# Finished rows stored from ScalarE's queue, the seventh page loaded by SyncE, and the experts' weights behind it

## The chip, the cores and the metric

The kernel runs on one core of one Trainium2 chip. The metric is the device time of one execution in microseconds: 382.13 us, the median of 3 runs of the kernel before (381.15 to 383.65). A page of a profile shows one execution, taken by the hardware profiler.

## The reference

The input is x of 8 batches, 2496 positions and 256 channels. Stage one mixes the positions of each batch by a filter in the frequency domain; stage two sends every position ("token") to one of 8 experts, of which each keeps its 80 tokens of highest gate weight, and puts them through two layers. All other rows of the output are zero.

```python
X = np.fft.rfft(x, axis=1)
Y = X * (filt_r + 1j * filt_i)[None]
t = np.fft.irfft(Y, n=2496, axis=1).reshape(19968, 256)
logits = t @ w_gate                                # 8 experts
expert_idx = argmax(logits); gate_w = softmax(logits)[expert_idx]
out = zeros((19968, 256))
for e in range(8):                                 # the 80 best tokens of expert e
    h = np.maximum(t[tok_idx] @ w1[e], 0.0)        # 256 -> 1024
    out[tok_idx] = gate_w[tok_idx, None] * (h @ w2[e])   # 1024 -> 256
```

## The kernel before

The kernel never makes all 19968 mixed rows. It makes the filtered spectrum of every batch, computes the gate's logits from the spectrum, chooses the tokens, and only for the chosen ones makes the rows themselves.

**The main loop** (up to about 233 us of the profile) transforms the batches by matmuls, multiplies by the filter, and writes each batch's spectrum, 2.6 MB, to a scratch tensor yf in DRAM; the last batch's spectrum stays in SBUF (yt_t). The output is zeroed by 32 stores in between.

**The rounds.** Behind the loop the chosen rows are made in seven rounds (NR) of up to 128 rows. Rounds 0 to 3 serve batches 0 to 3, one each; rounds 4 to 6 serve batches 4 to 7 in twelve groups of 32 rows, four groups to a round. For a round, GpSimd gathers rows of a table of cosines and sines by an indirect DMA (gather_rows, line 853, four for each round), VectorE turns them (turn_rows, line 864), and TensorE multiplies them with the "page" of the batch, the spectrum fetched back from yf into SBUF by four DMAs of 640 KB (load_page, line 838). `fill(n)` (line 876) issues the next n of a round's 20 steps. Round 5 takes rows of batches 5 and 6, round 6 of batches 6 and 7. At a round's end ScalarE copies the 128 finished rows out of PSUM (yr, one buffer; the tile z in round 5) and a DMA stores them to y_sel in DRAM (line 883).

**The experts** (function experts): the rows of each expert are gathered from y_sel by an indirect DMA (80 rows of 1 KB), turned by TensorE (px), and put through layer 1 (ph, line 1221) and layer 2 (po, line 1241); a scaled copy on ScalarE and an indirect DMA put them into the output. The first two experts' rows are gathered ahead (xg_first, line 1161), from the rounds 0 to 5 alone; the rows of round 6, still in SBUF, are added to them by a second matmul (line 1201). The others (xg_True, line 1188) are gathered from all of y_sel, the third expert's first. Expert 2's rows are turned in the middle of expert 0's layer 2 (`layer2(e, mid=lambda: turn(2))`).

**Weights.** w1 and w2 of an expert are 1 MB each, and each pair is fetched by two DMAs of SyncE (load_weights, lines 1066 and 1068) into one tile. The table WT names the buffer of each expert: its own tile, or the buffer of a page that its round has used up.

**What sets the order.** The work behind the loop is written under a manual schedule: each engine runs its instructions in the order in which the lines are written, and waits only for data and buffers. SyncE, ScalarE and GpSimd each issue DMAs on a queue of their own, in their own order; a DMA instruction that waits for data or a buffer holds up what stands behind it on its engine.

Of the kernel before, what the change touches and what calls it, by code (L numbers as in the profile page):

```python
# [13 lines left out]
F32 = mybir.dt.float32  # L14
# [5 lines left out]
B, S, C = 8, 2496, 256  # L20
# [13 lines left out]
E, FF = 8, 1024  # L34
NDB, NFC = C // 128, FF // 128
# [62 lines left out]
def kernel(  # L98
# [160 lines left out]
    with tc.manual_schedule():  # L259
# [608 lines left out]
        def fill(n):  # L868
            for _ in range(n):
# [9 lines left out]
                if s == NS - 1:  # L879
                    yr = (zs[:].rearrange("p e s -> p (e s)") if r == NR - 2 else  # L880
                          yr_p.tile([128, C], F32, name=f"yr_{r}", tag="yr"))
                    nc.scalar.copy(out=yr[:], in_=st["po"][:])  # L882
                    nc.sync.dma_start(
                        out=y_sel[128 * r:128 * r + 128, :], in_=yr[:])
                    st["yr"] = yr
# [164 lines left out]
        for name in ("t2", "pr", "fwd"):  # L1050
# [9 lines left out]
              (w_p, "w"), (last, "page"), (late, "page0")]  # L1060
        ws = {}

        def load_weights(e):
            where, tag = WT[e]
            ws[e] = where.tile([128, NDB * FF + NFC * C], F32, name=f"w_{e}", tag=tag)
            nc.sync.dma_start(out=ws[e][:, 0:NDB * FF].rearrange("p (k f) -> p k f", k=NDB),
                              in_=moe_w1[e].rearrange("(k p) f -> p k f", p=128))
            nc.sync.dma_start(out=ws[e][:, NDB * FF:].rearrange("p (k d) -> p k d", k=NFC),
                              in_=moe_w2[e].rearrange("(k p) d -> p k d", p=128))
# [3 lines left out]
        load_weights(0)  # L1073
# [23 lines left out]
        fill(2)  # L1097
# [10 lines left out]
        fill(7)  # L1108
# [5 lines left out]
        fill(13)  # L1114
        load_page(5, pg_p)
        load_weights(1)
# [17 lines left out]
        load_page(6, late, "page1", eng=nc.gpsimd)  # L1134
# [5 lines left out]
        fill(20)  # L1140
        turn_all(4)
# [13 lines left out]
        fill(10)  # L1155
        turn_all(6)
# [9 lines left out]
        for e in (3, 4):  # L1166
            load_weights(e)
# [13 lines left out]
    def experts(fp, psF, load, first):  # L1181
# [27 lines left out]
        def layer1(e, between=None):  # L1209
            w1 = ws[e][:, 0:NDB * FF].rearrange("p (k f) -> p k f", k=NDB)  # L1210
# [20 lines left out]
        def layer2(e, mid=None):  # L1231
            w2 = ws[e][:, NDB * FF:].rearrange("p (k d) -> p k d", k=NFC)
# [46 lines left out]
        for e in range(E):  # L1279
# [17 lines left out]
            n = e + 5 if first else e + 3  # L1297
# [12 lines left out]
    def general(tc, gctx):  # L1310
# [63 lines left out]
        def load(e):  # L1374
            ws[e] = wpool.tile([128, NDB * FF + NFC * C], F32, name=f"w2_{e}", tag="w")
            nc.sync.dma_start(out=ws[e][:, 0:NDB * FF].rearrange("p (k f) -> p k f", k=NDB),
                              in_=moe_w1[e].rearrange("(k p) f -> p k f", p=128))
            nc.sync.dma_start(out=ws[e][:, NDB * FF:].rearrange("p (k d) -> p k d", k=NFC),
# [415 lines left out]
```

## Time and profile before

| what | us |
| --- | --- |
| median of 3 runs | 382.13 |
| the profiled execution | 381.79 |
| its span, first to last instruction | 379.9 |
| TensorE busy | 352.4 |
| VectorE busy | 240.6 |
| GpSimd busy | 181.0 |
| ScalarE busy | 132.9 |

All times of the trace count from the span's start. PE is TensorE's matmul, PEld its weight load, DVE VectorE, ACT ScalarE, POOL GpSimd, SP SyncE; SPq and ACTq are the DMA issues of an engine. The names in the rows are the program's, with buffer numbers left out: gt are gathered rows of the table, wt the same rows turned, pr a round's sums in PSUM. A bracket behind a row tells how long the engine had been idle before it, and what released it. A float32 matmul shows as two rows of the trace.

### The profile page before, as it was taken

The numbers are of one execution on the slowest core, as the hardware profiler recorded it, in microseconds if no ns is written. First come the engines' busy times: TensorE is split into PE (matmuls) and PEld (weight loads), VectorE is DVE, ScalarE is ACT, GpSimd is POOL, SyncE is SP. The second block draws the span as 40 slices with busy tenths as digits, with TensorE's granted clock in tenths as the row PEclk, the third lists the DMA queues.
The fourth block names the chain that finished last, engine by engine and source line by source line (L and its number), as shares of the span: only waits on it lengthen the run. The fifth ranks groups of instructions, "written<-read, shape, count | busy, mean of one in ns | idle before, by whom it ended". The sixth has DMA issues, their size and how long they took to land. (4 is left out here: it accounts for less than half of the span.)

```text
span 379.9 us, 9671 instructions
## 1 busy us (share of the span) xinstructions
PE 352.4 (93%) x3941; PEld 312.5 (82%) x3941; DVE 240.6 (63%) x493; ACT 132.9 (35%) x275; POOL 181.0 (48%) x251
## 2 busy tenths in 40 slices
PE   8789999999999999999999999989899795997890
PEld 4789989989999899899899898778787363997880
DVE  6088666748868768789989887689947630121110
ACT  1445544554455455455354454150100000010110
POOL 8428455545545546646448858840283104022220
PEclk9999999999999999999999999999999998799997
DMA  7998698999989999989999999799999675989210
GB/s 220 282 340 262 207 331 263 321 305 305 346 274 303 369 265 326 333 235 310 348 295 271 394 296 335 270 405 388 416 406 399 222 249 166 332 286 363 88 31 12
DMA packets 41099, 109.92 MB, mean 289 GB/s; under 512 B 4202, under 2 KB 14312, under 8 KB 39176
## 3 DMA queue, kind: packets, MB, share of 16 engines
q1 hardware_dynamic: 36534, 95.94, 74.6%
q0 software_dynamic: 4240, 13.15, 9.7%
q8 instruction: 33, 0.54, 0.6%
q10 hardware_dynamic: 274, 0.14, 0.2%
q14 instruction: 18, 0.15, 0.1%
HBM read 70.42 MB, written 40.37 MB: 292 GB/s over the span
## 5 line engine op out<-in xcount | busy, mean ns | idle before, releaser
L360 POOL TENSOR_TENSOR yt<-p 128x256 f32<-128x256 f32 x157 | 113.6, 745 | 90.7 <-DVE p L352 87.4
L352 DVE TENSOR_TENSOR p<-pb,ft 128x1024 f32<-128x1024 f32 x80 | 97.0, 1215 | 42.1 <-issue 17.9
L316 PE MATMUL pa<-wf_t,x 117*128 117x120 f32 x704 | 90.6, 275 | 2.7 <-DMA x<-in_x_dram 1.8
L316 PEld LDWEIGHTS pa<-wf_t,x 117*128 117x128 f32 x704 | 84.5, 192 | 4.1 <-DMA x<-in_x_dram 1.4
L342 PE MATMUL pb<-d_t,t 128*128 128x128 f32 x640 | 84.7, 275 | 0.1
L342 PEld LDWEIGHTS pb<-d_t,t 128*128 128x128 f32 x640 | 77.8, 192 | 0.3 <-ACT t L335 0.3
L321 ACT COPY tt<-pa 128x480 f32<-128x480 f32 x96 | 47.9, 516 | 78.1 <-PE pa L316 77.0
L876 PE MATMUL pr<-page,wt 128*32 128x256 f32 (+1 forms) x520 | 64.5, 380 | 1.3 <-DVE wt L864 1.3
L876 PEld LDWEIGHTS pr<-page,wt 128*32 128x32 f32 (+1 forms) x520 | 46.4, 134 | 15.3 <-DVE wt L864 2.8
L335 ACT COPY t<-pt 128x512 f32<-128x512 f32 x80 | 47.2, 590 | 14.6 <-PE pt L331 12.6
L373 DVE STREAM_TRANSPOSE u<-yt 128x512 f32<-128x512 f32 x70 | 48.9, 699 | 0.0
L331 PE MATMUL pt<-ident,tt 128*128 128x128 f32 x320 | 48.6, 274 | 0.4 <-ACT tt L321 0.4
L853 POOL DMA_INDIRECT gt<-rows_tbl,idxr x28 | 29.8, 1064 | 33.9 <-DVE idxr L695 18.1
L331 PEld LDWEIGHTS pt<-ident,tt 128*128 128x128 f32 x320 | 37.3, 142 | 1.9 <-issue 1.2
L864 DVE STREAM_TRANSPOSE wt<-gt 128x640 f32<-128x640 f32 x28 | 22.7, 830 | 10.6 <-DMA gt<-rows_tbl,idxr 10.5
L1177 POOL DMA_INDIRECT out_dram<-ys_True,idxs x7 | 6.5, 933 | 34.8 <-ACT ys_True L1266 21.2
L396 PE MATMUL pz<-yt,wg 128*32 128x128 f32 (+1 forms) x256 | 21.9, 436 | 0.0
L882 ACT COPY yr<-pr 128x256 f32<-128x256 f32 x6 | 2.3, 380 | 54.9 <-PE misc L816 25.5
L1241 PE MATMUL po_True<-hT_True,w 128*64 128x80 f32 x448 | 17.9, 234 | 3.3 <-issue 3.3
L1221 PE MATMUL ph_True<-xs_True,w 128*64 128x80 f32 x512 | 20.9, 243 | 0.0
L1221 PEld LDWEIGHTS ph_True<-xs_True,w 128*64 128x64 f32 x512 | 20.0, 146 | 0.3 <-issue 0.2
L1241 PEld LDWEIGHTS po_True<-hT_True,w 128*64 128x64 f32 x448 | 16.3, 137 | 4.4 <-issue 3.8
(226 smaller groups left out, 287.4 us busy)
## 6 DMA issues: line engine op xcount, KB each, us to landing
out_dram<-zero_t SPq DMA_DIRECT2D x32, 624.0 KB
yf<-u SPq DMA_DIRECT2D x56, 320.0 KB, 5.3
w<-in_moe_w_dram SPq DMA_DIRECT2D x16, 1024.0 KB, 9.6
page<-yf SPq DMA_DIRECT2D x24, 640.0 KB, 9.5
x<-in_x_dram SPq DMA_DIRECT2D x16, 936.0 KB
x<-in_x_dram SPq DMA_DIRECT2D x7, 702.0 KB
page<-yf POOLq DMA_DIRECT2D x4, 640.0 KB, 8.7
fst<-in_filt_r_dram SPq DMA_DIRECT2D x10, 128.0 KB, 3.8
```

What stands on the lines that cost most here:

```text
L316: nc.tensor.matmul(out=ps[:, j, :], rhs=wf_t, start=True, stop=True, lhsT=xt[3 * b + ch][:, j0 + j - JC * ch, 128 * cb:128 * cb + 128])
L321: nc.scalar.copy(out=tt[h][:, :, H3 * j0:H3 * j0 + hn * jn].rearrange("p s (j h) -> p s j h", h=hn), in_=v)
L331: nc.tensor.transpose(ps[:, i, :], tt[h][:, 2 * s:2 * s + 2, :].rearrange("p r n -> p (r n)"), ident[:])
L335: nc.scalar.copy(out=t2[k][:], in_=ps[:])
L342: nc.tensor.matmul(out=ps[:, :, i, :], lhsT=t[:, i, :], rhs=d_t[:, SG * g + i, :], start=True, stop=True)
L352: nc.vector.tensor_tensor(out=p[:], in1=f.unsqueeze(2).to_broadcast(shape), op=AL.mult, in0=ps[:].rearrange("p r s q -> p r (s q)").unsque ...
L360: eng.tensor_tensor(out=y[:, :, 2 * r:2 * r + 2, :], in0=a, in1=b, op=op)
L373: nc.vector.transpose(uu[h][:, :, SG * g:SG * g + SG, :].rearrange("p a s w -> p s a w"), spectrum(h)[:, SG * g:SG * g + SG])
L853: nc.gpsimd.indirect_dma_start(out=gts[b, g][:].rearrange("p s q -> p (s q)"), out_offset=None, in_=quarters, in_offset=bass.IndirectOffse ...
L876: nc.tensor.matmul(st["po"][c:c + w, :], lhsT=wts[r][:, s, c:c + w], rhs=yt_t[:, :, s] if b == B - 1 else columns(pages[b], s), start=(s = ...
L1221: nc.tensor.matmul(ph[c:c + 64, i, 0:cap], lhsT=w1[:, k, f:f + 64], rhs=xs[:, k, :], start=(k == 0), stop=(k == NDB - 1))
L1241: nc.tensor.matmul(po[c:c + 64, d, 0:cap], lhsT=w2[:, fc, 128 * d + c:128 * d + c + 64], rhs=hT[:, fc, :], start=(fc == 0), stop=(fc == NF ...
```

## The change

- The store of a round's finished rows is issued by ScalarE, right behind its copy, and no longer by SyncE.
- The seventh page (of batch 6) is loaded by SyncE and no longer by GpSimd.
- The weights of expert 0 are loaded behind the seventh page and no longer ahead of the rounds; those of experts 1 to 5 stand behind rounds 3 to 6.
- Expert 5's weights get buffers of their own: its two halves lie in the two buffers of turned rows (pool u). Experts 6 and 7 take the buffers of experts 0 and 1 instead of 1 and 2.
- Four steps of round 1 stand ahead of the keys' turn to PSUM instead of behind it (fill 2, 7, 13 becomes 6, 5, 11).

```diff
@@ fill
                     nc.scalar.copy(out=yr[:], in_=st["po"][:])
-                    nc.sync.dma_start(
+                    nc.scalar.dma_start(
                         out=y_sel[128 * r:128 * r + 128, :], in_=yr[:])
@@ behind the loop
         WT = [(w_p, "w"), (last, "page"), (late, "page0"), (pg_p, "page"), (late, "page1"),
-              (w_p, "w"), (last, "page"), (late, "page0")]
+              None, (w_p, "w"), (last, "page")]
         ws = {}
 
         def load_weights(e):
-            where, tag = WT[e]
-            ws[e] = where.tile([128, NDB * FF + NFC * C], F32, name=f"w_{e}", tag=tag)
-            nc.sync.dma_start(out=ws[e][:, 0:NDB * FF].rearrange("p (k f) -> p k f", k=NDB),
+            if WT[e] is None:
+                ws[e] = [u_p.tile([128, NDB * FF], F32, name=f"w_{e}_{i}", tag="u")[:]
+                         for i in range(2)]
+            else:
+                where, tag = WT[e]
+                w = where.tile([128, NDB * FF + NFC * C], F32, name=f"w_{e}", tag=tag)
+                ws[e] = w[:, 0:NDB * FF], w[:, NDB * FF:]
+            nc.sync.dma_start(out=ws[e][0].rearrange("p (k f) -> p k f", k=NDB),
                               in_=moe_w1[e].rearrange("(k p) f -> p k f", p=128))
-            nc.sync.dma_start(out=ws[e][:, NDB * FF:].rearrange("p (k d) -> p k d", k=NFC),
+            nc.sync.dma_start(out=ws[e][1].rearrange("p (k d) -> p k d", k=NFC),
                               in_=moe_w2[e].rearrange("(k p) d -> p k d", p=128))
 
         load_page(2, late, "page1", nc.vector.memset)
         load_page(3, last)
-        load_weights(0)
...
-        fill(2)
+        fill(6)
         load_page(4, late, "page0")
...
         threshold(B, cap, 0)
-        fill(7)
+        fill(5)
         threshold(B, cap, "all")
...
         kept, rcnt, cnt = mark(B)
-        fill(13)
+        fill(11)
         load_page(5, pg_p)
-        load_weights(1)
...
-        load_page(6, late, "page1", eng=nc.gpsimd)
+        load_page(6, late, "page1")
+        load_weights(0)
         turn_all(3, (3, 4))
...
         fill(20)
+        load_weights(1)
         turn_all(4)
...
         fill(10)
+        load_weights(3)
         turn_all(6)
...
         fill(20)
-        for e in (3, 4):
-            load_weights(e)
+        load_weights(4)
+        load_weights(5)
@@ experts
-            n = e + 5 if first else e + 3
+            n = e + 6 if first else e + 3
             if n < E:
                 load(n)
```

The load of expert 2 keeps its place behind round 4. In layer1 and layer2 the two halves are addressed as ws[e][0] and ws[e][1]; the fallback branch, which these inputs do not take, is written in the same form.

How the change moves DMA issues is seen in two places. The first is GpSimd's queue behind the gathers of round 4: gt_0_3390 before (gt_0_3384 in the changed kernel) is round 4's last gather, the next three are round 5's, and page_3407 is the seventh page. Before:

```order
L853 DMA gt_2_3386<-rows_tbl,idxr 128x640
L853 DMA gt_0_3390<-rows_tbl,idxr 128x640
L838 DMA page_3407<-yf_151 128x1280 x4
L853 DMA gt_1_3413<-rows_tbl,idxr 128x640
L853 DMA gt_2_3417<-rows_tbl,idxr 128x640
L853 DMA gt_0_3421<-rows_tbl,idxr 128x640
```

And with the change:

```order
L853 DMA gt_2_3380<-rows_tbl,idxr 128x640
L853 DMA gt_0_3384<-rows_tbl,idxr 128x640
L853 DMA gt_1_3410<-rows_tbl,idxr 128x640
L853 DMA gt_2_3414<-rows_tbl,idxr 128x640
L853 DMA gt_0_3418<-rows_tbl,idxr 128x640
```

The page has left GpSimd's queue; round 5's gathers follow those of round 4 directly.

The second place is SyncE's queue from the sixth page (of batch 5) to the experts. Before, w_3236, w_3591, w_3847 and w_3850 are the weights of experts 1, 2, 3 and 4, and the stores to y_sel are those of rounds 2 to 6:

```order
L838 DMA page_3231<-yf_150 128x1280 x4
L1066 DMA w_3236<-in_moe_w_dram 128x2x1024
L1068 DMA w_3236<-in_moe_w_dram 128x8x256
L883 DMA y_sel<-yr_3404 128x256
L883 DMA y_sel<-yr_3458 128x256
L883 DMA y_sel<-yr_3588 128x256
L1066 DMA w_3591<-in_moe_w_dram 128x2x1024
L1068 DMA w_3591<-in_moe_w_dram 128x8x256
...
L883 DMA y_sel<-z 128x256
L883 DMA y_sel<-yr_3844 128x256
L1066 DMA w_3847<-in_moe_w_dram 128x2x1024
L1068 DMA w_3847<-in_moe_w_dram 128x8x256
```

With the change SyncE has pages and weights alone (page_3401 is the seventh page, w_3406 to w_3850 are experts 0 to 4, w_0_3853 and w_1_3854 the halves of expert 5):

```order
L838 DMA page_3228<-yf_150 128x1280 x4
L838 DMA page_3401<-yf_151 128x1280 x4
L1071 DMA w_3406<-in_moe_w_dram 128x2x1024
L1073 DMA w_3406<-in_moe_w_dram 128x8x256
L1071 DMA w_3458<-in_moe_w_dram 128x2x1024
...
L1071 DMA w_3748<-in_moe_w_dram 128x2x1024
L1073 DMA w_3748<-in_moe_w_dram 128x8x256
...
L1071 DMA w_3850<-in_moe_w_dram 128x2x1024
L1073 DMA w_3850<-in_moe_w_dram 128x8x256
L1071 DMA w_0_3853<-in_moe_w_dram 128x2x1024
L1073 DMA w_1_3854<-in_moe_w_dram 128x8x256
```

And the stores stand on ScalarE, each behind its copy; here the first round's and, behind it, the copy of the keys (kt), then the last two:

```order
L882 COPY yr_3100<-pr_2991 128x256
L883 DMA y_sel<-yr_3100 128x256
L489 COPY kt<-pk_3122 128x3x128
...
L882 COPY z<-pr_3653 128x256
L883 DMA y_sel<-z 128x256
L882 COPY yr_3847<-pr_3766 128x256
L883 DMA y_sel<-yr_3847 128x256
```

Before, the last store stood on SyncE ahead of the weights of experts 3 and 4; now those of experts 4 and 5 are issued by SyncE at the end of the same round, and the store by ScalarE behind its copy.

## Rows read from the trace of the kernel before

**Rows 1.** The page: busy time, share and instructions of TensorE; TensorE's granted clock in 40 slices of the span, in tenths; the queue of instruction fetches with packets, MB and share of the DMA engines.

```profile
PE 352.4 (93%) x3941; PEld 312.5 (82%) x3941; DVE 240.6 (63%) x493; ACT 132.9 (35%) x275; POOL 181.0 (48%) x251
...
PEclk9999999999999999999999999999999998799997
...
q8 instruction: 33, 0.54, 0.6%
```

**Rows 2.** Windows of 2 us: stretch, length, then busy us (and instructions) of PE, PEld, DVE, ACT and POOL, granted clock, DMA share, GB/s.

```profile
318.00:320.00 2.00, 1.09 (x8) 0.97 (x8) 0.33 (x1) 0.00 (x0) 0.36 (x1) 1.00 0.83 196
320.00:322.00 2.00, 0.16 (x1) 0.16 (x1) 0.00 (x0) 0.00 (x0) 1.53 (x2) 0.56 1.02 373
324.00:326.00 2.00, 2.00 (x34) 2.00 (x34) 0.20 (x1) 0.00 (x0) 0.00 (x0) 0.50 1.12 327
326.00:328.00 2.00, 2.00 (x48) 2.00 (x46) 0.11 (x1) 0.44 (x1) 0.00 (x0) 0.74 1.06 341
...
348.00:350.00 2.00, 0.65 (x19) 0.64 (x20) 0.00 (x0) 0.00 (x0) 0.00 (x0) 1.00 1.03 364
```

**Rows 3.** TensorE's timeline at the start of round 5: start, us, line, operation, tiles, shape, count, idle time before.

```profile
293.77 0.62 PE L876 MATMUL pr<-page,wt 128*32 128x256 f32 x2
...
296.96 4.50 PE L876 MATMUL pr<-page,wt 128*32 128x256 f32 x74 [0.43 <-DVE wt L864]
```

**Rows 4.** VectorE's timeline: the last turn of round 4's rows, the end of the weights' chain, and the last of the four turns of round 5's rows.

```profile
283.39 0.84 DVE L864 STREAM_TRANSPOSE wt<-gt 128x640 f32<-128x640 f32 x1 [0.37 <-DMA gt<-rows_tbl,idxr]
...
290.89 0.56 DVE L738 TENSOR_TENSOR eval<-gs,ehot 128x384 bf16<-128x384 bf16 x1
...
296.06 0.85 DVE L864 STREAM_TRANSPOSE wt<-gt 128x640 f32<-128x640 f32 x1 [0.21 <-DMA gt<-rows_tbl,idxr]
```

**Rows 5.** GpSimd's timeline: the four loads of the seventh page, and the gather of round 5's last rows.

```profile
277.75 2.20 POOL L838 DMA_DIRECT2D page<-yf  x4
...
284.26 1.16 POOL L853 DMA_INDIRECT gt<-rows_tbl,idxr  x1 [0.30 <-DVE wt L864]
```

**Rows 6.** DMA answers of short stretches: one issue each and its us to landing (the gather of 284.26; the second expert's gather of 316.98; the third expert's of 319.64; the last expert's of 351.52); then the two data queues in 290 to 300 us, with packets, MB and share of the 16 engines.

```profile
gt<-rows_tbl,idxr POOLq DMA_INDIRECT x1, 11.8
...
xg_first<-y_sel,idxg POOLq DMA_INDIRECT x1, 4.8
...
xg_True<-y_sel,idxg POOLq DMA_INDIRECT x1, 7.1
...
xg_True<-y_sel,idxg POOLq DMA_INDIRECT x1, 4.6
...
q1 hardware_dynamic: 1289, 1.73, 48.9%
q0 software_dynamic: 506, 1.73, 46.4%
```

**Rows 7.** TensorE's timeline from the last matmul of round 6 to the turn of the third expert's rows.

```profile
316.19 0.39 PE L876 MATMUL pr<-yt,wt 128*32 128x256 f32 x3
318.37 0.42 PE L1199 MATMUL px_True<-ident,xg_first 80*128 80x80 f32 x2 [1.78 <-DMA xg_first<-y_sel,idxg]
...
321.84 0.72 PE L1199 MATMUL px_True<-ident,xg_first 80*128 80x80 f32 x2 [2.39 <-DMA xg_first<-y_sel,idxg]
...
323.77 6.21 PE L1221 MATMUL ph_True<-xs_True,w 128*64 128x80 f32 x128
329.82 1.27 PE L1241 MATMUL po_True<-hT_True,w 128*64 128x80 f32 x32
331.02 0.36 PE L1204 MATMUL px_True<-ident,xg_True 80*128 80x80 f32 x2
```

**Rows 8.** SyncE's queue: issue time and us of the stores of rounds 0, 5 and 6.

```profile
252.46 8.61 SPq L883 DMA_DIRECT2D y_sel<-yr  x1
...
308.44 0.34 SPq L883 DMA_DIRECT2D y_sel<-z  x1
317.12 0.33 SPq L883 DMA_DIRECT2D y_sel<-yr  x1
```

**Rows 9.** GpSimd's timeline: the gathers of the first expert's rows and of the third expert's.

```profile
315.71 0.97 POOL L1161 DMA_INDIRECT xg_first<-y_sel,idxg  x1 [17.53 <-DMA y_sel<-z]
...
319.64 0.94 POOL L1188 DMA_INDIRECT xg_True<-y_sel,idxg  x1 [1.72 <-PE px_True L1201]
```

**Rows 10.** TensorE's timeline: one layer 1, and the three places in layer 2 where it stood and the trace puts it to "issue".

```profile
332.46 2.38 PE L1221 MATMUL ph_True<-xs_True,w 128*64 128x80 f32 x64
...
342.47 0.84 PE L1241 MATMUL po_True<-hT_True,w 128*64 128x80 f32 x18 [0.33 <-issue]
...
349.35 1.05 PE L1241 MATMUL po_True<-hT_True,w 128*64 128x80 f32 x24 [1.74 <-issue]
...
355.71 1.20 PE L1241 MATMUL po_True<-hT_True,w 128*64 128x80 f32 x29 [1.21 <-issue]
```

**Rows 11.** ScalarE's timeline: the copies of the finished rows of rounds 0, 1 and 6, and that of the keys.

```profile
252.01 0.42 ACT L882 COPY yr<-pr 128x256 f32<-128x256 f32 x1
252.86 0.87 ACT L489 COPY kt<-pk 128x384 f32<-128x384 f32 x1 [0.43 <-PE pk L487]
...
267.96 0.37 ACT L882 COPY yr<-pr 128x256 f32<-128x256 f32 x1 [13.33 <-DMA y_sel<-yr]
...
316.72 0.37 ACT L882 COPY yr<-pr 128x256 f32<-128x256 f32 x1 [8.30 <-PE pr L876]
```

More of the change, by code (lines that the diff above doesn't have):

```diff
@@ L1209, in layer1 @@
         def layer1(e, between=None):
-            w1 = ws[e][:, 0:NDB * FF].rearrange("p (k f) -> p k f", k=NDB)
+            w1 = ws[e][0].rearrange("p (k f) -> p k f", k=NDB)
             xs = xss.pop(e)
@@ L1231, in layer2 @@
         def layer2(e, mid=None):
-            w2 = ws[e][:, NDB * FF:].rearrange("p (k d) -> p k d", k=NFC)
+            w2 = ws[e][1].rearrange("p (k d) -> p k d", k=NFC)
             hT = hTs.pop(e)
@@ L1374, in load @@
         def load(e):
-            ws[e] = wpool.tile([128, NDB * FF + NFC * C], F32, name=f"w2_{e}", tag="w")
-            nc.sync.dma_start(out=ws[e][:, 0:NDB * FF].rearrange("p (k f) -> p k f", k=NDB),
+            w = wpool.tile([128, NDB * FF + NFC * C], F32, name=f"w2_{e}", tag="w")
+            ws[e] = w[:, 0:NDB * FF], w[:, NDB * FF:]
+            nc.sync.dma_start(out=ws[e][0].rearrange("p (k f) -> p k f", k=NDB),
                               in_=moe_w1[e].rearrange("(k p) f -> p k f", p=128))
-            nc.sync.dma_start(out=ws[e][:, NDB * FF:].rearrange("p (k d) -> p k d", k=NFC),
+            nc.sync.dma_start(out=ws[e][1].rearrange("p (k d) -> p k d", k=NFC),
                               in_=moe_w2[e].rearrange("(k p) d -> p k d", p=128))
```

## The prediction

> **What bounds the kernel now.** I read the page first, then TensorE's clock by windows, then the timelines of TensorE, VectorE, GpSimd, ScalarE and SyncE from 240 us on, and last the DMA answers for single issues. On the page [rows 1] the reader is to see that TensorE is busy for 352.4 us of a span of 379.9, so about 27 us can be won by removing waits, and that its clock sags in one place before the end, the 34th and 35th of 40 slices of 9.5 us. The windows [rows 2] show that place: the granted clock is 1.00 (2.4 GHz) until 320 us, falls to 0.50 (1.2 GHz) after 2 us in which TensorE did almost nothing (0.16 us busy), and is at 0.74 on its way back in 326 to 328. The main loop up to 233 us has the same instructions in the same order in both kernels, so all terms lie behind it, where TensorE runs its own instructions strictly in order. Three waits matter.
>
> First, round 5. Its first matmuls wait for turned rows [rows 3]: they begin at 293.77 and the steady run begins at 296.96, 3.19 us for six matmuls that take 0.06 us each at the steady rate (74 in 4.50 us), so 2.8 us are lost. VectorE shows why [rows 4]: it is free at 291.45 (290.89 + 0.56), but the four turns wait for gathered rows and the last ends at 296.91. GpSimd and the landing of one issue show why the rows are late [rows 5, 6]: the four loads of the seventh page stand in its queue at 277.75, ahead of round 5's gathers, and the gather issued at 284.26 lands 11.8 us later.
>
> Second, the passage from the last round to the experts. The last matmul of round 6 ends at 316.58 (316.19 + 0.39), and the first expert's layer 1 begins at 323.77 [rows 7]; in between lie two waits of 1.78 and 2.39 us, and the fall of the clock. TensorE waits there for the first two gathers from y_sel, and these wait for the store of round 5's rows: SyncE issued it at 308.44 and GpSimd was released by it at 315.71 [rows 8, 9], 7.27 us later, with two megabytes of expert 2's weights ahead of it on SyncE's queue.
>
> Third, three stalls in layer 2 that the trace puts to "issue", 0.33, 1.74 and 1.21 us, 3.28 together [rows 10]. They lie 127 matmuls apart by the counts of the timeline, and the instruction queue moves 0.54 MB in 33 packets [rows 1], 16 KB each, so I read them as waits for the next block of instructions behind weight traffic.
>
> **The change part by part.** Times are in the profiled execution (381.79 us); it stands 0.34 below the median of the runs, 382.13, from which I subtract at the end.
>
> *The seventh page on SyncE.* GpSimd loses four issues, 2.20 us with a gap of 0.3 [rows 5], so round 5's gathers go out 2.5 us earlier and no longer have 2.6 MB ahead of them in their own queue. They share the engines with the page and expert 0's weights; the queue shares of 290 to 300 us [rows 6] show two loaded queues at 48.9% and 46.4%, so half the engines remain for them. If all rows are there when VectorE is free, the turns take 4 x 0.84 from 291.45 and end at 294.81: 2.10 us gained. If round 4's gathers also land sooner, VectorE's chain moves up (its turns ended at 284.23, [rows 4]) and the whole 2.8 goes. I take **2.5**, since page 5 is fetched before round 4's gathers now and no longer beside them; bounds 2.1 and 2.8. Late next is VectorE's own chain of weights and slots.
>
> *Stores on ScalarE's queue.* Seven issues of 0.32 to 0.34 us [rows 8] become as many on ScalarE, 2.3 us on an engine that mostly idles there. One place counts: the first store comes ahead of the copy to kt, which feeds the threshold chain. The copy of yr begins at 252.01 and takes 0.42, so the store nearly fits in before 252.86, when kt's copy began [rows 11]; 0 to 0.3 us, I take 0. Round 1's copy, which waited 13.33 us for the first store [rows 11], is freed, but nothing on TensorE waited for it. The store of round 5's rows now flies beside expert 3's weights, which SyncE issues at the same matmul's end. Its landing lies between 2.52 us (the last store, issued at 317.12, had landed when GpSimd gathered at 319.64 [rows 8, 9]) and today's 7.27. Round 5 ends 2.5 us earlier, so the store goes out at 305.9; at 3.5 us GpSimd gathers at 309.4 and 310.7, and even the second gather (4.8 us to land, [rows 6]) is there at 315.5, when the turns need it.
>
> *What is late next.* Expert 2's gather needs the store of round 6, and its turn stands in the middle of expert 0's layer 2. Today: 0.54 us from the last matmul to the store's issue (316.58 to 317.12), landing 2.52, gather 7.1 [rows 6], so 326.7, while the turn comes only at 331.02 [rows 7]: 4.3 us to spare. After the change TensorE would reach that turn sooner. From the end of round 6: 2.0 for ScalarE's copy (done 0.51 behind it, [rows 11]) and two turns, 4.76 for two layers 1 (64 matmuls in 2.38, [rows 10]), 1.27 for half a layer 2 [rows 7], 8.0 in all. The rows are there only after 0.54 + store + gather. Today's store stood ahead of the weights in one queue; now SyncE sends four megabytes (experts 4 and 5) at the last matmul, half a microsecond ahead of it. At half the engines 0.13 MB takes under 1 us more, so I take 3.5 for the store (bounds 2.52 and 7.27) and 7.1 for the gather, which flew beside four megabytes of weights today too (bounds 4.6 and 7.1, [rows 6]). That is 11.1 us where it was 14.44 (316.58 to 331.02): **3.3** gained; bounds 6.4 gained (TensorE's own 8.0) and 0.5 lost.
>
> The Trainium skill bears on these stores. Its first page, "Trainium Kernel Development and Optimization", Key Constraints, says that DMAs from SyncE, ScalarE and GpSimd run on the same 16 engines and that issuing from several saves issue time alone; by that the sum would be the third rival's. "DMA: Bandwidth & Descriptors", Queues, rings and completion order, says that each DMA engine takes turns between the queues that have work; with that the queue shares above agree.
>
> *Weights.* Expert 0's go behind the seventh page, the others each behind the round or expert that frees their buffer, experts 4 and 5 at round 6's end. At some 330 GB/s, as in 324 to 328 us [rows 2], the last 8 MB from 314 on take 25 us and are done near 340; expert 4's layer 1 begins some 22 us behind expert 0's, when its first two megabytes have long landed. I cost the order of the weights at 0, with a bound of 2 if round 4's gathers suffer from the page. But the stalls of [rows 10] lay under the last three weight loads, 333 to 354 us. Today six block borders fall in loaded time from 320 to 355 us, 0.55 each; afterwards about three, so 1.6 remain and **1.6** are gained; bounds 3.3 gained and 1.9 lost (three of 1.74 us).
>
> Sum: 2.5 + 3.3 + 1.6 = 7.4 us; 382.13 - 7.4 = **374.7**.
>
> **Rivals.** *The rows come in time.* With 2.52 and 4.6 for store and gather the turn does not wait and TensorE's own 8.0 decides: 2.5 + 6.4 + 1.6 = 10.5, 371.6. For it speaks the store's 2.52, against it the 7.1 of today's gather for the same turn. *The clock falls in the new wait.* TensorE would stand for some 3 us before expert 2's turn; today the clock fell in a stretch with waits of 1.78 and 2.39 [rows 7]. The price is today's: from 321.84 to 326 at 0.50, 2.1 us lost, and 0.74 for 2 us, 0.5: 2.6 in all, 377.3. Against it: a wait of 1.74 us left it at 1.00 [rows 2, 10]. *ScalarE's queue gives no earlier landing* (the change does not do what it says): both stores take 7.27, the second term becomes a loss of 0.5, and 2.5 - 0.5 + 1.6 leaves 3.6, 378.5. Against it speak the queue shares [rows 6]. *Slower:* the last store is starved. Today's first store, issued at 252.46 behind pages and weights, was waited for until 267.96 [rows 8, 11], 15.5 us; if the four megabytes sent ahead of the last one hold it as long, 0.54 + 15.5 + 7.1 = 23.1 stands against 14.44, 8.7 lost, with 4.1 gained elsewhere: 386.7. It decides once store and gather take over 18.0 us (14.44 - 0.54 + 4.1). The same shares speak against it.
>
> **The numbers.** Chances: forecast 0.40, rows in time 0.15, clock 0.25, no earlier landing 0.15, starved 0.05. About 1%, 3.8 us, is what a measurement of this kernel can tell from no change. Below 378.3 us lie the first three nearly whole and some of the fourth, 0.84; within 1%: 0.11; slower by over 1%: 0.05. The range, 371.0 to 379.0, reaches from just under the case in which the rows come in time to just over the one of no earlier landing; the unknown stores and stalls leave out more at both ends, no more than 2 in 10.
>
> **What would show it.** Round 5's steady run should begin at most 1 us behind its first matmul; the store of round 5's rows should release GpSimd within 5 us; TensorE should then wait 2 to 4 us for expert 2's rows in the middle of expert 0's layer 2, a wait that today's trace does not have; the clock should be at 1.00 from round 6 into layer 1; the stalls put to "issue" should sit before 340 us. I am wrong if that wait is absent (then the kernel is faster), if the clock shows 0.50 behind it, or if the stores take 7 us as today.

## The result and the profile after

The changed kernel takes 384.03 us (median of 20 runs, 380.95 to 386.10) beside 381.13 (20 runs, 379.49 to 383.65) for the kernel before: a ratio of 1.0077, 95% interval 1.0053 to 1.0101. It is slower by 0.8%, where 374.7 us was forecast. All ratios leave out executions over 1.5% above the fastest of their kernel, so that a ratio can differ from that of the medians. The profiled execution took 385.27 us, its span is 383.2.

The page of the changed kernel: TensorE's busy time, its granted clock in 40 slices, and ScalarE's queue q10, which now carries the stores (packets, MB, share of the 16 engines; before it had 274 packets and 0.14 MB).

```profile
PE 355.1 (93%) x3941; PEld 315.8 (82%) x3941; DVE 240.5 (63%) x493; ACT 133.2 (35%) x275; POOL 178.6 (47%) x247
...
PEclk9999999999999999999999999998999997799997
...
q10 hardware_dynamic: 1282, 1.06, 0.9%
```

The same matmuls are 2.7 us longer busy than in [rows 1]. The clock sags deeper in the slices of [rows 1], and once more before them, in the 28th (0.59 in 258 to 262 us); some 1.5 us are lost there (an estimate from TensorE's busy time in these windows) and the rest mainly in the later place. TensorE's timeline of the changed kernel shows that place (start, us, line, tiles, count, idle time before):

```profile
296.77 0.80 PE L748 MATMUL pe_s<-eval,eplc 128*80 128x56 bf16 x16
297.49 4.52 PE L876 MATMUL pr<-page,wt 128*32 128x256 f32 x80
...
316.75 0.39 PE L876 MATMUL pr<-yt,wt 128*32 128x256 f32 x3
321.37 0.69 PE L1205 MATMUL px_True<-ident,xg_first 80*128 80x80 f32 x2 [4.23 <-DMA xg_first<-y_sel,idxg]
...
324.59 0.71 PE L1205 MATMUL px_True<-ident,xg_first 80*128 80x80 f32 x2 [1.25 <-DMA xg_first<-y_sel,idxg]
...
326.51 6.51 PE L1227 MATMUL ph_True<-xs_True,w 128*64 128x80 f32 x128
...
334.06 0.36 PE L1210 MATMUL px_True<-ident,xg_True 80*128 80x80 f32 x2
```

Round 5 now runs straight through its 80 matmuls, without the wait of [rows 3]. But the passage from round 6 to the experts, 7.19 us in [rows 7] (316.58 to 323.77), is 9.37 now (317.14 to 326.51): the first wait grew from 1.78 to 4.23 us. The turn of expert 2's rows (L1210) follows without a wait. ScalarE's and SyncE's queues and GpSimd's timeline of the changed kernel give the reason; the two stores first, then SyncE's weights of experts 3 and 4 issued about them, then the gathers that wait for the stores:

```profile
309.00 0.35 ACTq L883 DMA_DIRECT2D y_sel<-z  x1
...
317.64 0.35 ACTq L883 DMA_DIRECT2D y_sel<-yr  x1
```

```profile
308.54 0.37 SPq L1071 DMA_DIRECT2D w<-in_moe_w_dram  x1
...
317.15 0.38 SPq L1071 DMA_DIRECT2D w<-in_moe_w_dram  x1
```

```profile
316.60 0.97 POOL L1167 DMA_INDIRECT xg_first<-y_sel,idxg  x1 [18.28 <-DMA w<-in_moe_w_dram]
...
324.26 0.94 POOL L1194 DMA_INDIRECT xg_True<-y_sel,idxg  x1 [5.44 <-DMA y_sel<-yr]
```

The store of round 5's rows takes 7.60 us from issue to gather (309.00 to 316.60; [rows 8, 9]: 7.27), that of round 6's 6.62 (317.64 to 324.26; [rows 8, 9]: 2.52 at most). The first gather's bracket names a weight load, which landed after the store; but by the landings in the traces this gather starts 0.86 to 1.04 us behind the last part of its store in every run, and the third expert's 0.78, so it is the store that releases both. Of the 2.45 us by which the first wait grew the store has only 0.3: the gather itself took 4.77 us to TensorE's start (316.60 to 321.37), where it took 2.66 before (315.71 to 318.37, [rows 7, 9]). The DMA queues in single microseconds show what the first one waits for. The stretches are 309 to 310, 312 to 313 and 313 to 314 us; q1 is SyncE's queue, q10 ScalarE's; columns are packets, MB and share of the 16 engines.

```profile
q1 hardware_dynamic: 276, 0.32, 109.0%
...
q1 hardware_dynamic: 122, 0.40, 100.4%
q10 hardware_dynamic: 13, 0.01, 3.8%
...
q1 hardware_dynamic: 127, 0.28, 71.6%
q10 hardware_dynamic: 104, 0.10, 28.5%
```

For three microseconds behind its issue not one packet of the store moves; SyncE's queue has the engines for itself. Of its 144 packets 117 pass in these last two stretches and the rest behind them. The windows of the changed kernel show what the long wait does to the clock (columns as in [rows 2]):

```profile
318.00:320.00 2.00, 0.00 (x0) 0.00 (x0) 0.00 (x0) 0.00 (x0) 0.82 (x1) 1.00 0.85 189
320.00:322.00 2.00, 0.63 (x3) 0.66 (x4) 0.00 (x0) 0.00 (x0) 0.00 (x0) 0.55 1.00 390
322.00:326.00 4.00, 2.75 (x14) 2.53 (x13) 0.32 (x1) 0.00 (x0) 1.43 (x2) 0.50 1.09 357
326.00:328.00 2.00, 2.00 (x25) 1.85 (x26) 0.32 (x1) 0.00 (x0) 1.40 (x2) 0.50 1.04 416
328.00:330.00 2.00, 2.00 (x34) 2.00 (x33) 0.00 (x0) 0.44 (x1) 0.00 (x0) 0.50 1.05 333
```

It falls behind 2 us with no matmul at all (318 to 320) to 0.50, which is 1.2 GHz, and is still there in 328 to 330, where in [rows 2] it was on its way back by 326.

### The profile page after: what moved, and what is told of

Its sections match the earlier page's. It is cut to its first block, busy times and chain, and to the rows that moved or that the text cites. A ratio compares the mean times of both kernels' runs of the same rounds, so it can differ in the third digit from the quotient of the medians.

```text
span 383.2 us, 9665 instructions
## 1 busy us (share of the span) xinstructions
PE 355.1 (93%) x3941; PEld 315.8 (82%) x3941; DVE 240.5 (63%) x493; ACT 133.2 (35%) x275; POOL 178.6 (47%) x247
## 5 line engine op out<-in xcount | busy, mean ns | idle before, releaser
L876 PEld LDWEIGHTS pr<-page,wt 128*32 128x32 f32 (+1 forms) x520 | 47.7, 137 | 14.7 <-issue 2.8
L373 DVE STREAM_TRANSPOSE u<-yt 128x512 f32<-128x512 f32 x70 | 48.9, 699 | 0.0
L1227 PE MATMUL ph_True<-xs_True,w 128*64 128x80 f32 x512 | 22.8, 246 | 1.9 <-issue 1.9
L1227 PEld LDWEIGHTS ph_True<-xs_True,w 128*64 128x64 f32 x512 | 21.1, 148 | 3.0 <-issue 2.9
L396 PEld LDWEIGHTS pz<-yt,wg 128*32 128x32 f32 x256 | 8.5, 109 | 12.3 <-issue 7.4
```

What stands on the lines that cost most here:

```text
L373: nc.vector.transpose(uu[h][:, :, SG * g:SG * g + SG, :].rearrange("p a s w -> p s a w"), spectrum(h)[:, SG * g:SG * g + SG])
L396: nc.tensor.matmul(out=ps[32 * j:32 * j + 32].rearrange("p (s w) -> p s w", s=pn), lhsT=wg[:, cb, :], rhs=yt_t[:, (2 * b + cb) % 2, 5 * j ...
L876: nc.tensor.matmul(st["po"][c:c + w, :], lhsT=wts[r][:, s, c:c + w], rhs=yt_t[:, :, s] if b == B - 1 else columns(pages[b], s), start=(s = ...
L1227: nc.tensor.matmul(ph[c:c + 64, i, 0:cap], lhsT=w1[:, k, f:f + 64], rhs=xs[:, k, :], start=(k == 0), stop=(k == NDB - 1))
```

## The experiments

For each run I read four stretches from TensorE's timeline and ScalarE's first copy: A from that copy of round 0's ranks (249.64 in the kernel before) to row_index (pb_r); B from there to the end of round 6; C from there to the first layer 1; D from there to the end of the last matmul. Times in us, ratios with their 95% intervals; the kernel before was timed beside each group of runs (medians 381.13, then 378.68 for e1 to e4, 381.07 for e5 to e8, 380.83 for e9 to e12), and each of these three groups ran on a chip of its own.

| kernel | ratio | A | B | C | D |
|---|---|---|---|---|---|
| before, first profile | 1 | 20.85 | 46.09 | 7.19 | 47.23 |
| changed, first profile | 1.0077 | 22.70 | 45.17 | 9.37 | 47.67 |
| e1 stores on SyncE | 0.987 (0.9804-0.9935) | 20.90 | 43.78 | 7.41 | 46.52 |
| e2 | 0.9995 (0.9969-1.0021) | 20.89 | 43.81 | 8.69 | 46.63 |
| e3 | 0.9956 (0.9925-0.9987) | 20.89 | 43.79 | 5.65 | 48.88 |
| e4 | 1.0047 (1.0018-1.0076) | 20.85 | 44.93 | 8.32 | 46.10 |
| e5 | 0.9977 (0.9945-1.001) | 22.73 | 45.22 | 2.80 | 48.95 |
| e6 | 0.9945 (0.9921-0.997) | 22.28 | 45.41 | 3.57 | 48.67 |
| e7 | 1.0045 (1.0017-1.0073) | 22.62 | 45.22 | 10.00 | 46.59 |
| e8 | 1.0138 (1.011-1.0165) | 22.72 | 48.80 | 3.65 | 47.81 |
| e9 before again | 0.9983 (0.9954-1.0013) | 22.27 | 48.20 | 2.23 | 48.87 |
| e10 changed again | 1.0086 (1.0049-1.0123) | 22.65 | 45.23 | 10.06 | 46.44 |
| e11 as e1 | 0.9947 (0.9914-0.998) | 22.16 | 45.23 | 6.08 | 47.96 |
| e12 | 1.0242 (1.02-1.0284) | 22.21 | 56.30 | 2.23 | 48.93 |

A profile is one execution, a ratio ten to twenty (four in e1, e8 and e12); they need not agree to the last microsecond.

**e1: all stores back on SyncE.**

```diff
-                    nc.scalar.dma_start(
+                    nc.sync.dma_start(
                         out=y_sel[128 * r:128 * r + 128, :], in_=yr[:])
```

> The changed kernel with the seven stores back on SyncE's queue, at the same places of the program, so that the store of round 5 stands ahead of expert 3's weights and that of round 6 ahead of those of experts 4 and 5. Both theories, that the store is held by the weights issued half a microsecond ahead of it, and that ScalarE's queue is served later whatever flies, expect the round 5 store to land within 4 us (7.6 in the changed kernel), layer 1 of expert 0 to begin 3 to 5 us sooner than there (326.5), and a time of 379 to 381. If the stores are slow for a third reason, their landing stays at 6 to 8 us and the time at 384.

Measured: 376.22 us, 0.987, from four executions. Without ScalarE's queue the change is a gain here. But round 5's store still took 7.16 us (304.49 to 311.65), which neither theory expected; round 6's releases GpSimd within 4.3 us instead of 6.6.

**e2: expert 3's weights written behind round 6's matmuls, stores on ScalarE.**

```diff
         fill(10)
-        load_weights(3)
         turn_all(6)
...
         fill(20)
+        load_weights(3)
         load_weights(4)
```

> The changed kernel with the load of expert 3's weights moved behind round 6, stores left on ScalarE's queue. If the store of round 5 is slow because it starts beside expert 3's weights, it lands within 4 us now, the first gathers go out some 4 us sooner and layer 1 of expert 0 begins by 322.5: time 379 to 381. If ScalarE's queue is slow by itself, the store still takes 6 to 8 us and the time stays at 383 to 385.

Measured: 379.07 us, 0.9995. The test failed as a test: SyncE has nothing before that load that it waits for, and issued it at 306.79, at the end of round 5 as in the changed kernel. It is the changed kernel almost unaltered, with 7.0 us for both stores; what it added to the study is that A was 20.89 here and not 22.7, and that on this chip the change is no loss (0.9995).

**e3: both edits.** On SyncE the store of round 6 stands ahead of the moved load and holds it back.

> Both edits, stores on SyncE's queue and expert 3's weights behind round 6. With the theory of flight: round 5's store lands in about 2.5 us, the first gathers are there before round 6 ends, round 6's store goes out ahead of the weights: time 377 to 380. With the theory of the slow queue this equals the run with the stores alone on SyncE, within 1 us.

Measured: 377.64 us, 0.9956. The load went out at 316.11, behind round 6, and C fell to 5.65; but round 5's store still took 7.18 us with no weights issued behind it. The edit of e3 against e1 is expert 3's weights alone, and what it shortened is the first gather, from issue to TensorE's start: 4.79 us in e1 (311.65 to 316.44), 2.69 in e3 (314.18 to 316.87). D grew by 2.4 us over e1, in waits of 0.65, 1.09, 1.46 and 1.74 us that the trace puts to "issue": six megabytes of weights now follow round 6.

**e4: the fills of the kernel before, 2, 7 and 13 steps.**

```diff
-        fill(6)
+        fill(2)
...
-        fill(5)
+        fill(7)
...
-        fill(11)
+        fill(13)
```

> The changed kernel with the steps of rounds 0 and 1 in the order of before (fill 2, 7, 13). If the four steps put ahead of the keys' turn delay ScalarE's copies and with them the threshold chain, the copy to kt begins at about 253 (254.36 in the changed kernel), row indices end at about 272.0 instead of 273.45 and the time falls by 1 to 1.5, to about 382.5. If the delay comes from the store in front of the copy to kt, the copy stays at 254.0 or later and the time is the same as the changed kernel's, 384.

Measured: 380.62 us, 1.0047. The new fills don't cost the time: with the old ones B is 1.1 us longer than in e1 to e3, and the median 1.6 us above that of e2.

**e5: round 6's store on SyncE, expert 3's weights behind it; round 5's store stays on ScalarE.**

```diff
-                    nc.scalar.dma_start(
+                    (nc.sync if r == NR - 1 else nc.scalar).dma_start(
...
-        load_weights(3)
         turn_all(6)
...
         fill(20)
+        load_weights(3)
         load_weights(4)
```

> The changed kernel with the last store (round 6's) issued by SyncE and expert 3's weights behind it, so that SyncE really holds them back; round 5's store stays on ScalarE's queue with only expert 2's weights in flight on SyncE's. Theory of the forecast (a second queue gets half the engines): round 5's store releases GpSimd within 4 us, TensorE's first wait for px shrinks below 1 us, and round 6's end to the first layer 1 takes 5 to 5.5 us. Rival (a store waits for the weight bytes in flight, whichever queue it is on): round 5's store takes about 7 us again, as the one behind expert 2's weights on SyncE's queue did, and only the last store falls from 6.6 to about 2.5 us; round 6's end to layer 1 about 6 to 7. By the first the kernel takes about 0.985 of before, by the second 0.99 to 1.00.

Measured: 380.2 us, 0.9977; C is 2.80. ScalarE's queue and GpSimd's timeline of e5:

```profile
309.42 0.33 ACTq L883 DMA_DIRECT2D y_sel<-z  x1
```

```profile
315.19 0.97 POOL L1166 DMA_INDIRECT xg_first<-y_sel,idxg  x1 [17.18 <-DMA y_sel<-z]
```

The DMA queues of e5 in 309 to 310, 310 to 311, 312 to 313 and 313 to 314 us:

```profile
q1 hardware_dynamic: 290, 0.30, 84.1%
...
q1 hardware_dynamic: 198, 0.20, 58.1%
q10 hardware_dynamic: 90, 0.08, 23.9%
...
q1 hardware_dynamic: 24, 0.02, 6.9%
q10 hardware_dynamic: 2, 0.00, 0.3%
...
q1 hardware_dynamic: 10, 0.01, 2.6%
q10 hardware_dynamic: 9, 0.01, 2.4%
```

The store takes 5.77 us, between the two theories' 4 and 7, but the rows speak against the forecast's: it gets nothing in the first stretch, in which SyncE's queue holds 84% of the engines, its packets pass as expert 2's weights drain, and the last nine, a sixteenth of the store, come on about one engine's share, beside the last 34 weight packets (312 to 314). Yet TensorE waits only 0.37 us for the first gather: with no weights behind the store, GpSimd's gathers fly alone. So C is shorter than even the first theory had it, by moving the weights and not by the queue. What is gained comes back in part as D (plus 2.5 us against e10): stalls put to "issue" of up to 1.54 us.

**e6: all stores on SyncE, expert 2's weights behind round 5's store, expert 3's behind round 6's.**

```diff
         fill(20)
-        load_weights(2)
         turn_all(5)
...
         fill(10)
-        load_weights(3)
+        load_weights(2)
         turn_all(6)
...
         fill(20)
+        load_weights(3)
         load_weights(4)
```

> The changed kernel with all stores on SyncE and expert 2's weights behind round 5's store, expert 3's behind round 6's, so that nothing but the tail of expert 1's weights is in flight when round 5's store goes out. If the seven microseconds of that store are weight bytes ahead of it, it now releases GpSimd within 3 us, the first px doesn't wait (under 0.5 us) and round 6's end to layer 1 takes about 4.5 to 5.5 us. If the seven microseconds are a fixed cost of something else (a shared completion semaphore, GpSimd itself), they stay at 6.5 to 7.5. What it costs: six megabytes behind round 6 instead of four, so the experts' stalls may grow to some 5 us as where only expert 3's weights were late; the whole 0.985 to 0.998 of before.

Measured: 378.9 us, 0.9945. SyncE's queue, GpSimd's and TensorE's timeline of e6, and between them SyncE's DMA queue in 308 to 309 us:

```profile
307.96 0.34 SPq L883 DMA_DIRECT2D y_sel<-z  x1
```

```profile
q1 hardware_dynamic: 59, 0.06, 16.7%
```

```profile
310.66 0.97 POOL L1166 DMA_INDIRECT xg_first<-y_sel,idxg  x1 [14.51 <-issue]
```

```profile
318.00 0.42 PE L1205 MATMUL px_True<-ident,xg_first 80*128 80x80 f32 x2 [1.66 <-DMA xg_first<-y_sel,idxg]
```

With idle engines the store takes 2.70 us, and 59 packets have moved 1.04 us behind its issue. What goes beyond that in the seven microseconds is therefore weight bytes handed out before it, and no fixed cost. The expectation missed in the next step: the first px still waits 1.66 us, now for a gather that flies beside expert 2's weights.

**e7: round 0's store alone back on SyncE.**

```diff
-                    nc.scalar.dma_start(
+                    (nc.sync if r == 0 else nc.scalar).dma_start(
```

> The changed kernel with round 0's store alone back on SyncE. Theory: the store on ScalarE's queue held the fifth page's issue until it landed (SyncE waited 16.7 us for a landing there) and so made round 4 late; without it SyncE issues the fifth page behind the store without that wait, round 4 ends 43.4 to 43.7 us behind the first copy of round 0's ranks (47.5 in the changed kernel, 43.4 before), and the kernel gains 1.5 to 2.5 us on the changed one (about 1.001 to 1.004 of before where the changed one was 1.008). Rival: the late round 4 is no matter of this store (weights and pages compete whatever it does): round 4's end stays at 46 to 47.5 and the time at 1.005 to 1.010.

In the changed kernel SyncE stood before the fifth page for the landing of a store that the page doesn't read (waits of SyncE's queue, changed kernel):

```profile
SPq L838 <- DMA y_sel<-yr: 16.7, 1, 16.7
```

Measured: 382.51 us, 1.0045. The fifth page's first load went out at 255.36 here and at 262.20 in the changed kernel, so the hold was gone; yet A is 22.62, B 45.22 and round 4's last slots begin 47.5 us behind the first copy, all as in the changed kernel. That theory of mine fell: the hold doesn't set round 4's end.

**e8: the kernel before with its stores on ScalarE's queue, and nothing else.**

```diff
-                    nc.sync.dma_start(
+                    nc.scalar.dma_start(
                         out=y_sel[128 * r:128 * r + 128, :], in_=yr[:])
```

> The kernel before with only the seven stores moved to ScalarE's queue; the seventh page stays on GpSimd, weights where they were. Forecast's theory: both late stores land in 3.5 us, 3.3 us gained, 0.991 of before. Rival (the queue gives no earlier landing, and the last store loses its place ahead of the weights): round 5's store about 7 us, round 6's 6 to 7 us instead of 2.5, which the 4.3 us to spare before expert 2's turn just cover; the first store may hold the fifth page: 1.000 to 1.008 of before.

Measured: 385.66 us, 1.0138, worse than either theory had it (the span of its profiled execution is 381.1, so the table shows less of the loss than the median; where the rest lies is not shown). Round 6's store, issued at 322.27, releases GpSimd at 328.05, 5.8 us later. Round 5's store gives the plainest view of the queue: SyncE issued its weights at 312.32 and 312.75 into engines that were idle, ScalarE the store at 312.79, and the queues of e8 in 313 to 316, 316 to 317 and 317 to 318 us are

```profile
q1 hardware_dynamic: 165, 0.68, 81.4%
...
q1 hardware_dynamic: 98, 0.37, 90.8%
q10 hardware_dynamic: 22, 0.02, 6.3%
...
q1 hardware_dynamic: 271, 0.27, 75.8%
q10 hardware_dynamic: 122, 0.11, 31.4%
```

The megabyte issued first (packets of 4 KB: 0.68 MB in 165) passes nearly alone. Then the store passes, ahead of most of the second megabyte (packets of 1 KB), though that was issued 0.04 us before it: by 318 all 144 packets of the store are through and at most 271 of some 1024.

**e9, e10, e11: the kernel before, the changed kernel and e1 again, side by side.**

> The kernel before, unchanged, on the chip of the next three runs, as a control of the two upstream delays (the copies of the first ranks on ScalarE split by a gap of 1.5 to 2.2 us, row_index 22.3 to 22.7 us behind them where it was 20.85; and round 4's slots, pe_s, 24.8 us behind row_index where it was 22.55). These stood in the changed kernel and in four later runs, also with all stores on SyncE, and in none of the four runs before these. If they belong to the chip or the execution, this run shows them whenever the changed kernel beside it does, and its time is about 381; if they belong to the change, this run shows 20.85 and 22.55 and the changed kernel beside it shows the delays again.

> The changed kernel, unchanged, on the same chip. If the upstream delays are of the chip: they stand here and in the kernel before alike (or in neither), and the time differs from before by the passage alone, ratio 0.998 to 1.004. If they are of the change: 22.7 and 24.8 us here, 20.85 and 22.55 in the kernel before, ratio 1.006 to 1.010 again.

> The changed kernel with all stores on SyncE, a second time, beside the two controls. If ScalarE's queue is what cost the time, it is 0.983 to 0.993 of before again and 4 to 6 us below the changed kernel; the last store releases GpSimd about 2 us earlier than in the changed kernel. If the first reading was that chip's alone, it lies within 1% of the changed kernel.

Measured: 380.68, 384.71 and 380.44 us; 0.9983, 1.0086 and 0.9947. ScalarE's timeline of e9, the kernel before:

```profile
249.51 0.57 ACT L388 COPY yt<-pq 128x512 f32<-128x512 f32 x1
250.96 0.59 ACT L388 COPY yt<-pq 128x512 f32<-128x512 f32 x1 [0.88 <-PE pr L876]
```

The gap between these copies, which I had taken for a cost of the change, stands in the kernel before too, and A is 22.27. So A tells next to nothing of the change: it is 20.85 to 20.90 in all runs of e1 to e4 and 22.16 to 22.73 in all of e5 to e12, whatever the kernel; only within the second kind is it some 0.4 us longer with stores on ScalarE (22.62 to 22.73) than with all of them on SyncE (22.16 to 22.28). B must be compared within one kind: 46.09 against 43.8 in the first, 48.20 against 45.23 in the second. Of C, e9 and e10 tell most. SyncE's store, GpSimd's gather and TensorE's end of round 6 and first layer 1 in e9:

```profile
311.70 0.34 SPq L883 DMA_DIRECT2D y_sel<-z  x1
```

```profile
316.33 0.97 POOL L1161 DMA_INDIRECT xg_first<-y_sel,idxg  x1 [18.71 <-DMA y_sel<-z]
```

```profile
319.45 0.53 PE L876 MATMUL pr<-yt,wt 128*32 128x256 f32 x3
322.21 2.50 PE L1221 MATMUL ph_True<-xs_True,w 128*64 128x80 f32 x65
```

and GpSimd's two releases and TensorE's two waits in e10:

```profile
317.47 0.96 POOL L1167 DMA_INDIRECT xg_first<-y_sel,idxg  x1 [19.14 <-DMA w<-in_moe_w_dram]
...
325.01 0.94 POOL L1194 DMA_INDIRECT xg_True<-y_sel,idxg  x1 [5.32 <-DMA y_sel<-yr]
```

```profile
322.10 0.42 PE L1205 MATMUL px_True<-ident,xg_first 80*128 80x80 f32 x2 [4.07 <-DMA xg_first<-y_sel,idxg]
...
326.16 0.72 PE L1205 MATMUL px_True<-ident,xg_first 80*128 80x80 f32 x2 [2.97 <-DMA xg_first<-y_sel,idxg]
```

In e9 the store took 4.63 us, TensorE waited for no gathered row, and the clock stayed at 1.00 through the passage. In e10 the stores, issued at 309.89 and 318.52, took 7.58 and 6.49, and TensorE waited 7.04 us. In e11 GpSimd was released at

```profile
315.24 0.97 POOL L1167 DMA_INDIRECT xg_first<-y_sel,idxg  x1 [18.19 <-DMA w<-in_moe_w_dram]
...
321.42 0.94 POOL L1194 DMA_INDIRECT xg_True<-y_sel,idxg  x1 [3.96 <-PE px_True L1207]
```

6.49 us behind the store of 308.75 and 2.83 behind that of 318.59. The second bracket names TensorE; by the landings it was the store, 0.78 us before, as in every run. TensorE waited 3.32 us once. There the first two gathers left at 315.24 and 316.5, before SyncE issued the last weights (319.02); in e10 the second one left at 318.7, behind the first of them (318.04). So the same weights at the same places cost 4 us less in C (6.08 against 10.06) with the stores ahead of them in one queue than with a queue of their own, and 4.3 us by the medians.

**e12: the kernel before with the seventh page alone on SyncE.**

```diff
-        load_page(6, late, "page1", eng=nc.gpsimd)
+        load_page(6, late, "page1")
```

> The kernel before with the seventh page alone moved to SyncE; stores, weights and order as before. Forecast's first term alone: round 5's wait of 2.8 us goes or shrinks to under 0.7, GpSimd's gathers of round 5 go out 2.2 us earlier, 0.992 to 0.994 of before. Rival (SyncE issues the page behind stores and weights 0 and 1, so that it comes late or meets the gathers): the wait moves to the page or to round 4's rows, 0.998 to 1.005.

Measured: 389.76 us, 1.0242. SyncE reached the page at 288.76 only, behind expert 1's weights (286.29) and a store (287.28); GpSimd issued it at 277.75 [rows 5], and in e11 SyncE did at 278.08. TensorE's timeline of e12:

```profile
305.37 7.06 PE L876 MATMUL pr<-page,wt 128*32 128x256 f32 x76 [7.84 <-DMA page<-yf]
```

With expert 1's weights ahead of it the page on SyncE is a loss. In e1 and e11 the stores are on SyncE too, but the weights stand behind the page, and there is no such wait.

## Why the prediction was wrong

*The seventh page, 2.5 us gained: near in size, and the wait it names is gone.* Like against like, B shortened by 2.3 us (46.09 to 43.8) and 3.0 (48.20 to 45.23), but not all of that is the page. In the first kind 1.1 us of it go with the new fills (e4). In the second the wait of [rows 3] doesn't stand in the kernel before either: e9 waits in round 4 instead, and its clock fell there:

```profile
292.00:294.00 2.00, 2.00 (x24) 1.49 (x20) 1.63 (x2) 0.00 (x0) 0.00 (x0) 0.50 1.01 392
```

It was at 0.50 for 3.4 us from 291.6, so some 1.7 of the 3.0 us are the clock's (an estimate from these rows). That the sum came near 2.5 is in part luck. e12 shows that this term was the page's and the weights' together, and no gift of the page alone.

*The stores on ScalarE's queue, 3.3 us gained: the step that failed.* "At half the engines 0.13 MB takes under 1 us more, so I take 3.5" was wrong for both stores. They took 7.6 and 6.6 us (7.6 and 6.5 in e10); the third rival had 7.27 for both, and of the landings, not of the time, it came true. For round 5's store the queue made little difference: with expert 2's weights ahead of it it took 7.16, 7.18 and 6.49 us on SyncE's (e1, e3, e11) and 7.60, 7.58 and twice 7.0 on ScalarE's (changed, e10, e2, e4). I had read the queue shares of [rows 6], two queues at 48.9 and 46.4%, as what any queue gets beside another. Those were two queues with megabytes each. A store of eight rows per engine got nothing while earlier weights passed, in the changed kernel, in e5 and in e8. Strict service in the order of issue doesn't fit either: in e8 the store overtook the half of a weight load that was issued just before it. The rows fit turns between the queues that last at least as long as the half of such a load; I varied the order and the load, not the rule itself, so that reading is the simplest and not the only one. The Trainium skill, "DMA: Bandwidth & Descriptors", Queues, rings and completion order, has each DMA engine take turns between queues with work, a whole packet of descriptors at a time; the rows agree with turns, but show none as short as a microsecond (in the changed kernel 0 packets of the store beside 276, 213 and 158 of SyncE's in 309 to 312). The Trainium skill, "Trainium Kernel Development and Optimization", Key Constraints, says that a further issuing engine saves issue time alone; the 7.60 us beside 7.27 before agree. And the change took something away that I did cost, but as cheap: on SyncE round 6's store stood ahead of the weights and had 2.5 us; on ScalarE it was issued half a microsecond behind them.

The path was wrong as well. I had the passage's first two waits gone, with expert 2's turn as what is late next. In the changed kernel the first two gathers stayed late, expert 2's turn followed without a wait, and so round 6's slow store cost TensorE nothing there.

*The order of the weights, 0: the second step that failed.* I bounded it at 2 us, by round 4's gathers, and looked in the wrong place. Expert 3's weights moved from the end of round 6 to that of round 5, and there they fly beside round 5's store and its two gathers, for which the passage waits. e3, which takes them back out of e1, has the first gather at TensorE 2.1 us sooner behind its issue. e5, which takes these weights back out and has round 6's store on SyncE, has C of 2.80 against 10.06. This is what made the loss larger than the third rival's, which kept 3.6 us of gain: C and D together grew by 2.6 us from the first profile to the changed one, by 5.4 from e9 to e10, where the forecast had 4.9 gained and that rival 1.1 (1.6 less 0.5).

*The stalls put to "issue", 1.6 us gained: near in size, not in place.* They sum to 1.86 us where [rows 10] had 3.28, and to 2.02 in e10 against 5.27 in e9; in the first kind e2 has 2.34 and e1 3.14. The prediction had about three, before 340 us; the changed kernel has six of about 0.3 us between 341 and 357, so the size is in part luck. e3, e5 and e6, which send the weights later, sum to about 5 us each: weights sent early pay in C and gain in D. That the stalls wait for blocks of instructions was read from counts, and no run tests it.

*The clock.* My second rival had the fall behind expert 2's turn. It came at the first px wait and lasted longer than in the kernel before. From 321.37 to 330 some 7.4 us of TensorE's work ran at 0.50, so about 3.7 us were lost to it (an estimate from those windows), where [rows 2] cost 2.6.

*The fills and the first store's place, 0:* not at a cost, at least. e4 suggests 1.1 us gained by the new fills (one profile, and medians 1.6 apart), and e7 shows no gain in A or B outside what all runs beside it have.

Of the prediction's signs only the first came, round 5's straight run. The store released GpSimd after 7.6 us and not 5, expert 2's turn had no wait though the kernel was not faster, the clock fell in the passage, and the stalls came behind 340.

The net: 2.3 to 3.0 us gained in the rounds and 2.6 to 5.4 lost behind them. The share of A in the first two profiles, 1.85 us, was no effect of the change: e2, which runs nearly as the changed kernel does, has 20.89, and the kernel before has 22.27 in e9. e1 keeps the page, the buffers and the order of the weights as changed and leaves the stores on SyncE: 0.987 and, again, 0.9947 of before. The second of these is no more than e6 (0.9945) and e3 (0.9956) have, and its median is only 0.4 us under that of the kernel before.

## What to carry to other kernels

A small transfer that someone waits for is sped up by having fewer bytes handed out before it, not by a queue of its own: keep it ahead of the bulk loads in their queue, or hold those back until it and what it releases have landed. When a bulk load is moved earlier, ask which small store and gather it now flies beside. Before explaining a difference upstream of a change, profile the old kernel again beside the new one.

## What the hardware showed beyond that

A stretch with nearly the same instructions took two lengths, 20.9 us for all kernels of e1 to e4 and 22.2 to 22.7 for all of e5 to e12; in the longer one the trace shows one or two gaps of 0.8 to 2.2 us between copies on ScalarE, and why was not tried. A wait for a landing can come from an unrelated transfer: SyncE stood 16.7 us before a page until a store on another queue had landed, though nothing in the page needs that store; by the trace the page's first load waits for the semaphore which that store signals. And a sixteenth of a store can be late alone, it seems behind one engine with weights left to move, as in e5, where its last part landed 1.7 us behind the others.
